# Where GpSimd's table scatters and early gathers stand among the powers of the layer norm

## The chip, the cores and the metric

The kernel runs on one core of one Trainium2 chip. A core has five engines with a queue of instructions each: TensorE (PE, with its weight loads, PEld), VectorE (DVE), ScalarE (ACT), GpSimd (POOL) and SyncE (SP). Each takes its own instructions strictly in order, and an instruction that waits for a semaphore holds up everything behind it on its engine. The metric is device time in microseconds (us) for one execution; lower is better.

## The reference: what is computed

Three layers run in a row on 4 x 576 = 2304 tokens of width 512.

```python
# 1. attention, 4 x 8 heads, 576 x 64; half of the heads look at the last 32 positions,
#    the other half at every 32nd
attn = softmax(where(mask, q @ k.T / 8, -1e9)); x = attn @ v      # -> (2304, 512)
# 2. dense layer of width 1024 with a soft gate and a layer norm
h = x @ w_in
solu = h * softmax(h)
ln = (solu - mean(solu)) / sqrt(var(solu) + 1e-6) * g_ln
x = ln @ w_out
# 3. eight experts, one per token
logits = x @ w_gate + modality_bias[modality_id]
e_idx = argmax(logits); gate_w = softmax(logits)[e_idx]
out[t] = gate_w[t] * (relu(x[t] @ w1[e_idx[t]]) @ w2[e_idx[t]])
```

## The kernel before, in words

The tokens are cut into 18 tiles of 128. The loop over `t` near the end of the function drives everything up to the experts: attention is spread over it in small slots, and iteration `t` does the first half of tile `t` and the second half of tile `t - 1`.

*First half* (`moe_a`, L463 to L497). PE computes `ph`, the product with `w_in`, in two halves of 12 matmuls. DVE takes the maximum (`hmx`) and its negative (`hnb`), ACT the exponential `e`, DVE the product `so` with its row sum.

*Second half.* `moe_stats` (L499 to L515) makes the layer norm's factors: ACT's square of `so` gives `var`, DVE makes `rstd`, **GpSimd raises it to the power -0.5 (L510)**, and DVE makes `sc` (L512) and `nm` (L514) from it. `moe_b_front` flips `so` on PE (`pn`), and ACT and DVE split it into `nH` and `nL`. `moe_b` (L529) multiplies by `w_out` on PE, into two PSUM tiles `pa` and `pb` of a pool with two buffers for both; ACT scales them by `sc` into `yt` (L541, L542), and DVE reads the gate's columns out of `pa` as `LG` (L543). The next tile's `pa` can't be written before that `LG` has been read. `yt` goes to `y_d` in DRAM.

*Routing.* After tiles 5, 11, 15 and 17 a group of 6, 6, 4 or 2 tiles is routed. `route_a` finds each token's expert, `route_b` (L592) its row in a table, and GpSimd writes one table row per token with an indirect transfer, one *scatter* per tile (L610). All scatters write `tab_d`, so each waits until the one before it has landed. After tile 11 the kernel chooses the expert that has most tokens so far. SP loads the first part of its list of tokens (`idxE`, L746) from the table, and GpSimd fetches their rows of `y_d` with four *gathers* into `xgE` (L824), which PE flips (`px`) in the last iteration, so that the first expert can start on them.

The order on each engine is set by the scheduler of the tile framework: it orders instructions by their dependences and a simulated timeline. `queue_after` (L715) adds a dependence without a semaphore: on the same engine, the later one is to be issued behind the earlier one. In the program before, nothing of that kind stands on scatters, gathers or powers.

Of the kernel before, what the change touches and what calls it, by code (L numbers as in the profile page):

```python
# [23 lines left out]
def indirect(ap):  # L24
    return bass.IndirectOffsetOnAxis(ap=ap, axis=0)
# [3 lines left out]
def tile_attention_moe_moe2(  # L29
# [19 lines left out]
    P = 128  # L49
# [413 lines left out]
    def moe_a(t, front, between):  # L463
# [32 lines left out]
                so[:, hf], e[:, hf], 1.0, hs[hf], ALU.mult, ALU.mult, accum_out=a2[:, hf:hf + 1])  # L496
        return so, e, s2, a2  # L497

    def moe_stats(so, e, s2, a2):  # L499
        nmu = st.tile([P, 1], F32, name="nmu")  # L500
        nc.vector.tensor_scalar(nmu, a2[:, 0:1], a2[:, 1:2], -1.0 / FF, ALU.add, ALU.mult)
        var = st.tile([P, 1], F32, name="var")
        nc.scalar.activation(e, so, AF.Square, bias=nmu, scale=1.0, accum_out=var)
        rs = st.tile([P, 1], F32, name="rs")
        nc.vector.tensor_scalar(rs, s2[:, 0:1], s2[:, 1:2], 1e-9, ALU.add, ALU.add)
        nc.vector.reciprocal(rs, rs)
        rstd = st.tile([P, 1], F32, name="rstd")
        nc.vector.tensor_scalar(rstd, rs, rs, 1.0 / FF, ALU.mult, ALU.mult)
        nc.vector.tensor_scalar(rstd, rstd, var, 1e-6, ALU.mult, ALU.add)
        nc.gpsimd.tensor_tensor(rstd, rstd, mhalf, ALU.pow)  # L510
        sc = st.tile([P, 1], F32, name="sc")
        nc.vector.tensor_tensor(sc, rstd, rs, ALU.mult)  # L512
        nm = st.tile([P, 1], F32, name="nm")
        nc.vector.tensor_tensor(nm, sc, nmu, ALU.mult)  # L514
        return sc, nm  # L515
# [76 lines left out]
    def route_b(t0, t1, tmp, eb):  # L592
        n = t1 - t0
        s = slice(t0, t1)
        pr = ps.tile([P, 6, NE], F32, name="pr", tag="T")
        nc.tensor.matmul(pr[:, :n], upper, OH[:, s], start=True, stop=False)
        nc.tensor.matmul(pr[:, :n], ones, CUM[:, s], start=False, stop=True)
        nc.vector.tensor_tensor(tmp[:, :n], pr[:, :n], OH[:, s], ALU.mult)
        rk = st.tile([P, 6], F32, name="rk")
        nc.vector.reduce_sum(rk[:, :n], tmp[:, :n], axis=AX.X)  # L600
        lo = st.tile([P, 6], I32, name="rlo")
        nc.vector.tensor_copy(lo[:, :n], rk[:, :n])
        hi = st.tile([P, 6], I32, name="rhi")
        nc.vector.tensor_scalar(hi[:, :n], lo[:, :n], 7, None, ALU.logical_shift_right)
        nc.vector.tensor_scalar(lo[:, :n], lo[:, :n], P - 1, None, ALU.bitwise_and)
        nc.vector.tensor_tensor(hi[:, :n], hi[:, :n], eb[:, :n], ALU.add)
        pos = st.tile([P, 6], I32, name="rpos")
        nc.vector.scalar_tensor_tensor(pos[:, :n], lo[:, :n], NTC, hi[:, :n], ALU.mult, ALU.add)
        for t in range(t0, t1):
            nc.gpsimd.indirect_dma_start(  # L610
                out=tab_d[:, :], out_offset=indirect(pos[:, t - t0:t - t0 + 1]),
                in_=entry[:, t], in_offset=None)

    mpstack = ExitStack()
    mp = mpstack.enter_context(tc.tile_pool(name="mp", bufs=2, side="right"))
# [204 lines left out]
        return w[3][f] if isinstance(w[3], list) else w[3][:, f]  # L820

    def gather(x, idx, j, rows=NT + 1, blocks=(0, 1)):
        for b in blocks:
            nc.gpsimd.indirect_dma_start(  # L824
                out=x[:, b], out_offset=None, in_=y_d[0:rows, :],
                in_offset=indirect(idx[:, 2 * j + b, 0:1].bitcast(U32)))

    def transpose_x(x, blocks=(0, 1), shift=0):
        for b in blocks:
            p = ps.tile([P, KD, P], F32, name="px", tag="T")  # L830
            for c in range(KD):
                flip_tile(p[:, c], x[:, b, c * P:(c + 1) * P], ident)
            s = slice((b + shift) * P, (b + shift + 1) * P)
            cp = nc.scalar.copy(gH[:, :, s], p)
            dv = nc.vector.tensor_tensor(gL[:, :, s], p, gH[:, :, s].bitcast(F32), ALU.subtract)  # L835
        return cp, dv
# [175 lines left out]
    for t in range(NTILE + 1):  # L1012
        bt = min((P * t + P - 1) // S, B - 1)
        take(4 * (16 * (bt + 1) + LAG))
        if taken >= QMAX and not done_att:
            done_att = True
            next(slots, None)
            atstack.close()
            wfst = ctx.enter_context(tc.tile_pool(name="wfst", bufs=1))
            W[0] = (wfst.tile([P, KD, FF], F32R, name="w1H"), wfst.tile([P, KD, FF], F32R, name="w1L"),  # L1020
                    wfst.tile([P, KF, DM], F32R, name="w2H"),
                    [x[:, i, 0:DM] for x in (xTH, xTL) for i in range(4)])

        def slot_bg(n=0):
            between()
            for _ in range(n):
                if background and W[0]:
                    background.pop(0)()

        if t == NTILE - 1:  # L1030
            while background:
                background.pop(0)()
            for j in range(EARLY):
                xgE[j] = rawp.tile([P, 2, DM], F32, name=f"xgE{j}", tag="raw")
                gather(xgE[j], idxE, j, 1 + EARLY_T * P)
        nT = []

        def front():
            if state and not nT:
                nT.extend(moe_b_front(state[1][0]))  # L1040

        cur = None
        if state:
            stats = moe_stats(*state[1])
        if t < NTILE:
            cur = (t, moe_a(t, front, slot_bg))
            reading[0] = t + 1
        front()
        slot_bg(1)
        if t == NTILE - 1:  # L1050
            transpose_x(xgE[0])
        if state:
            d = state[0]
            while wout or unfused:
                if unfused:
                    fuse_gate(*unfused.pop(0))
                if wout:
                    unfused.append(prep_w_out(wout.pop(0)))
            if d == 0:
                column_sums()  # L1060
            moe_b(d, *nT, *stats, slot_bg)
            if routed:
                route_b(*routed.pop())
            if d in (5, 11):
                routed.append((d - 5, d + 1, *route_a(d - 5, d + 1)))
            elif d == 15:
                routed.append((12, 16, *route_a(12, 16)))
            if d == EARLY_T - 1:
                choose_first()
                e_first = load_reg(infoE[0:1, 1:2], NE - 1, engines=[SP])  # L1070
                background = weight_steps(0, e_first)
                background.pop(0)()
            if d == EARLY_T + 2:
                load_idx(idxE, e_first)
        slot_bg(1)
        state = cur
    rt = route_a(16, 18)
    yo = mp.tile([P, 2, DM], F32, name="yoE", tag="e")
    chunk256(W[0], idxE, 0, ahead=lambda: route_b(16, 18, *rt), then=lambda: transpose_x(xgE[1]))
    choose_rest()  # L1080
    mpstack.close()
    e_r = [e_first] + [load_reg(info[0:1, NE + i:NE + i + 1], NE - 1, engines=[SP]) for i in range(1, NE)]
# [186 lines left out]
```

## Time and profile before

| | |
|---|---|
| median of 3 runs | 666.09 us (664.16 to 667.23) |
| profiled execution | 665.19 us, of which the span of the profile is 663.5 us |
| PE busy | 613.0 us, 92% of the span |
| PE weight loads busy | 551.2 us, 83% |
| DVE busy | 368.0 us, 55% |
| ACT busy | 320.7 us, 48% |
| POOL busy | 169.9 us, 26% |
| mean granted clock of PE | 0.972 |

The span is the time from the first to the last instruction. Since PE is busy for most of it, an instruction on another engine counts only where PE waits for it. The wait tables say how long an engine stood idle and whose semaphore came last; a timeline gives the same for one instruction, in brackets. PEclk is the share of TensorE's full clock that was granted in a stretch. An engine's row without a bracket started with no idle time before it.

### The profile page before, as it was taken

The page shows a single profiled execution, that of the slowest core. Times are in us where ns is not written, and L with a number is a line of the kernel's source. Part 1 is how long each engine was busy: PE and PEld are TensorE (multiplying, and loading weights), DVE is VectorE, ACT ScalarE, POOL GpSimd, SP SyncE. Part 2 cuts the span into 40 slices and gives each one's busy share as a digit, 9 for nine tenths or more (in the row PEclk, how much of TensorE's full clock was granted, in tenths as well). Part 3 has the DMA queues.
Part 4 walks back from the last instruction along what each step waited for, and adds up shares of the span by engine and source line. Part 5 has one row for each costly group of instructions (what it writes and reads, how often), then busy time and mean ns, then how long its engine had stood idle before and what let it go on. Part 6 is the DMA issues. An engine that isn't in the chain of part 4 may idle for free. (4 is left out here: it accounts for less than half of the span.)

```text
span 663.5 us, 12578 instructions
## 1 busy us (share of the span) xinstructions
PE 613.0 (92%) x4536; PEld 551.2 (83%) x4536; DVE 368.0 (55%) x1152; ACT 320.7 (48%) x709; POOL 169.9 (26%) x224
## 2 busy tenths in 40 slices
PE   6777989999999999999999699999899998999992
PEld 5666878999899987988889599889788887899892
DVE  5898788577767857677388353224454642221120
ACT  4898666566655657666275232223425352221220
POOL 2426455012432342111023203210120304012011
PEclk9997979999999999999999799999999999999997
DMA  8758221034111212110044200253636462012010
GB/s 221 178 152 219 75 82 37 21 85 117 52 53 40 78 49 57 53 35 16 17 159 128 80 33 18 68 178 123 198 112 223 126 211 88 27 55 64 17 49 24
DMA packets 54771, 59.98 MB, mean 90 GB/s; under 512 B 39312, under 2 KB 39312, under 8 KB 54674
## 3 DMA queue, kind: packets, MB, share of 16 engines
q1 hardware_dynamic: 47810, 42.52, 22.9%
q0 software_dynamic: 4272, 11.57, 5.5%
q10 hardware_dynamic: 2592, 4.72, 1.9%
q8 instruction: 47, 0.77, 0.5%
q14 instruction: 50, 0.41, 0.2%
HBM read 49.05 MB, written 10.26 MB: 89 GB/s over the span
## 5 line engine op out<-in xcount | busy, mean ns | idle before, releaser
L856 PE MATMUL py<-w2H,winL 128*128 128x512 f32 x288 | 92.0, 395 | 0.0
L896 PE MATMUL pf<-xTH,w1H 128*128 128x256 f32 x288 | 82.2, 286 | 3.1 <-DVE yo L995 2.1
L896 PE MATMUL pf<-xTL,w1H 128*128 128x256 f32 x288 | 81.6, 283 | 0.3 <-DVE xTL L835 0.3
L896 PE MATMUL pf<-xTH,w1L 128*128 128x256 f32 x288 | 81.4, 283 | 0.0
L903 DVE SCALAR_TENSOR_TENSOR winL<-pf,winL 128x512 fp32r<-128x512 f32 x36 | 24.9, 692 | 96.2 <-ACT winL L902 96.1
L368 POOL TENSOR_TENSOR ex<-ex,rd 96x384 f32<-96x384 f32 (+1 forms) x56 | 47.7, 852 | 108.3 <-DVE rd L362 64.0
L327 PE MATMUL S<-kz,qT 128*72 128x72 f32 (+1 forms) x448 | 59.2, 281 | 8.6 <-ACT kz L311 6.7
L902 ACT ACTIVATE winL<-pf 128x512 fp32r<-128x512 f32 x36 | 21.6, 599 | 87.9 <-PE pf L896 86.2
L856 PEld LDWEIGHTS py<-w2H,winL 128*128 128x128 f32 x288 | 53.4, 188 | 10.5
L327 PEld LDWEIGHTS S<-kz,qT 128*72 128x72 f32 (+1 forms) x448 | 51.1, 179 | 12.3 <-ACT kz L311 8.4
L480 PE MATMUL ph<-winH,xTH 128*128 128x512 f32 x144 | 59.5, 413 | 1.1 <-ACT xTH L400 0.8
L896 PEld LDWEIGHTS pf<-xTH,w1H 128*128 128x128 f32 x288 | 56.1, 195 | 4.6 <-issue 2.6
L480 PE MATMUL ph<-winL,xTH 128*128 128x512 f32 x144 | 57.9, 402 | 0.0
L896 PEld LDWEIGHTS pf<-xTL,w1H 128*128 128x128 f32 x288 | 56.2, 195 | 0.8 <-DVE xTL L835 0.5
L480 PE MATMUL ph<-winH,xTL 128*128 128x512 f32 x144 | 56.8, 401 | 0.0
L896 PEld LDWEIGHTS pf<-xTH,w1L 128*128 128x128 f32 x288 | 56.2, 195 | 0.0
L862 POOL DMA_INDIRECT out_dram<-yo,idx x14 | 14.1, 1006 | 146.6 <-ACT yo L861 122.8
L536 PE MATMUL pa<-woH,nH 128*128 128x264 f32 x144 | 43.1, 299 | 7.5 <-DVE LG L543 6.3
L536 PE MATMUL pa<-woH,nL 128*128 128x264 f32 x144 | 43.5, 302 | 0.2 <-DVE nL L526 0.2
L346 POOL TENSOR_TENSOR ex<-ex,mx 96x384 f32<-96x384 f32 (+1 forms) x32 | 24.9, 779 | 69.6 <-DVE mx L342 41.1
L357 DVE TENSOR_REDUCE den<-ex 72x4 f32<-72x292 f32 (+1 forms) x64 | 31.7, 497 | 19.2 <-ACT ex L349 10.2
L536 PE MATMUL pa<-woL,nH 128*128 128x264 f32 x144 | 41.9, 291 | 0.0
(244 smaller groups left out, 1601.7 us busy)
## 6 DMA issues: line engine op xcount, KB each, us to landing
raw<-in_moe_w_dram SPq DMA_DIRECT2D x36, 512.0 KB, 4.1
y_d<-yt ACTq DMA_DIRECT2D x18, 256.0 KB, 2.1
raw<-in_moe_w_in_dram SPq DMA_DIRECT2D x8, 512.0 KB, 6.9
raw<-in_moe_w_out_dram SPq DMA_DIRECT2D x8, 512.0 KB
vn<-in_v_dram SPq DMA_DIRECT2D x16, 160.0 KB, 3.8
qn<-in_q_dram SPq DMA_DIRECT2D x8, 288.0 KB
kn<-in_k_dram SPq DMA_DIRECT2D x8, 288.0 KB
vn<-in_v_dram SPq DMA_DIRECT2D x8, 288.0 KB
```

The source lines that it names most:

```text
L327: nc.tensor.matmul(sp_[:nq, i, :nk], qT[:, q0:q0 + nq], kT[:, half, k0:k0 + nk], start=True, stop=True)
L346: eng.tensor_tensor(ex[:nq, :nt, :nk], ex[:nq, :nt, :nk], mx[:nq, :nt].unsqueeze(2).to_broadcast([nq, nt, nk]), ALU.subtract)
L357: nc.vector.reduce_sum(den[:nq, :nt], exw[:nq, :nt, EPS:EPS + 1 + nk], axis=AX.X)
L368: nc.gpsimd.tensor_tensor(ex[:nq, :nt, :nk], ex[:nq, :nt, :nk], rd[:nq, :nt].unsqueeze(2).to_broadcast([nq, nt, nk]), ALU.mult)
L480: nc.tensor.matmul(ph, a[:, c, ts_], w[:, c, cs], start=n == 0, stop=n == 3 * KD - 1)
L536: nc.tensor.matmul(p, a[:, f], w[:, f, cols], start=n == 0, stop=n == 3 * KF - 1)
L856: nc.tensor.matmul(p, a[:, f, s], x, start=n == 0, stop=n == 3 * KF - 1)
L862: nc.gpsimd.indirect_dma_start(out=out[:, :], out_offset=indirect(idx[:, col, 2:3].bitcast(U32)), in_=o, in_offset=None, bounds_check=NT - ...
L896: mm = nc.tensor.matmul(p[:, u], a[:, c, fs], x[:, c], start=n == 0, stop=n == 3 * KD - 1)
L902: last[0] = (nc.scalar.activation(hH[:, f2s], p, AF.Relu), nc.vector.scalar_tensor_tensor(hL[:, f2s], p, 0.0, hH[:, f2s].bitcast(F32), ALU ...
L903: nc.vector.scalar_tensor_tensor(hL[:, f2s], p, 0.0, hH[:, f2s].bitcast(F32), ALU.max, ALU.subtract))
```

## The change

Two things are given an issue order on GpSimd. First, `route_b` no longer issues its scatters itself; it returns them as a list, and the loop puts them on `owed`. In each iteration, right after `moe_stats`, up to three of them (four in the last) are issued, and each is tied behind the power of that iteration (`pow_`). The last group, tiles 16 and 17, is issued as before. Second, the four gathers of `xgE` move from ahead of `moe_stats` in iteration 17 to behind it, and each is tied behind that iteration's power, which is the power of tile 16.

```diff
--- before.py
+++ after.py
@@ -496,6 +496,9 @@
                 so[:, hf], e[:, hf], 1.0, hs[hf], ALU.mult, ALU.mult, accum_out=a2[:, hf:hf + 1])
         return so, e, s2, a2
 
+    pow_ = [None]
+    owed = []
+
     def moe_stats(so, e, s2, a2):
         nmu = st.tile([P, 1], F32, name="nmu")
         nc.vector.tensor_scalar(nmu, a2[:, 0:1], a2[:, 1:2], -1.0 / FF, ALU.add, ALU.mult)
@@ -507,7 +510,7 @@
         rstd = st.tile([P, 1], F32, name="rstd")
         nc.vector.tensor_scalar(rstd, rs, rs, 1.0 / FF, ALU.mult, ALU.mult)
         nc.vector.tensor_scalar(rstd, rstd, var, 1e-6, ALU.mult, ALU.add)
-        nc.gpsimd.tensor_tensor(rstd, rstd, mhalf, ALU.pow)
+        pow_[0] = nc.gpsimd.tensor_tensor(rstd, rstd, mhalf, ALU.pow)
         sc = st.tile([P, 1], F32, name="sc")
         nc.vector.tensor_tensor(sc, rstd, rs, ALU.mult)
         nm = st.tile([P, 1], F32, name="nm")
@@ -606,10 +609,17 @@
         nc.vector.tensor_tensor(hi[:, :n], hi[:, :n], eb[:, :n], ALU.add)
         pos = st.tile([P, 6], I32, name="rpos")
         nc.vector.scalar_tensor_tensor(pos[:, :n], lo[:, :n], NTC, hi[:, :n], ALU.mult, ALU.add)
-        for t in range(t0, t1):
-            nc.gpsimd.indirect_dma_start(
+        def scatter(t):
+            return nc.gpsimd.indirect_dma_start(
                 out=tab_d[:, :], out_offset=indirect(pos[:, t - t0:t - t0 + 1]),
                 in_=entry[:, t], in_offset=None)
+
+        return [lambda t=t: scatter(t) for t in range(t0, t1)]
+
+    def scatters(n):
+        for _ in range(n):
+            if owed:
+                queue_after(owed.pop(0)(), pow_[0])
 
     mpstack = ExitStack()
     mp = mpstack.enter_context(tc.tile_pool(name="mp", bufs=2, side="right"))
@@ -820,10 +830,11 @@
         return w[3][f] if isinstance(w[3], list) else w[3][:, f]
 
     def gather(x, idx, j, rows=NT + 1, blocks=(0, 1)):
-        for b in blocks:
+        return [
             nc.gpsimd.indirect_dma_start(
                 out=x[:, b], out_offset=None, in_=y_d[0:rows, :],
                 in_offset=indirect(idx[:, 2 * j + b, 0:1].bitcast(U32)))
+            for b in blocks]
 
     def transpose_x(x, blocks=(0, 1), shift=0):
         for b in blocks:
@@ -1030,9 +1041,6 @@
         if t == NTILE - 1:
             while background:
                 background.pop(0)()
-            for j in range(EARLY):
-                xgE[j] = rawp.tile([P, 2, DM], F32, name=f"xgE{j}", tag="raw")
-                gather(xgE[j], idxE, j, 1 + EARLY_T * P)
         nT = []
 
         def front():
@@ -1042,6 +1050,12 @@
         cur = None
         if state:
             stats = moe_stats(*state[1])
+            scatters(4 if t == NTILE else 3)
+        if t == NTILE - 1:
+            for j in range(EARLY):
+                xgE[j] = rawp.tile([P, 2, DM], F32, name=f"xgE{j}", tag="raw")
+                for x in gather(xgE[j], idxE, j, 1 + EARLY_T * P):
+                    queue_after(x, pow_[0])
         if t < NTILE:
             cur = (t, moe_a(t, front, slot_bg))
             reading[0] = t + 1
@@ -1060,7 +1074,7 @@
                 column_sums()
             moe_b(d, *nT, *stats, slot_bg)
             if routed:
-                route_b(*routed.pop())
+                owed.extend(route_b(*routed.pop()))
             if d in (5, 11):
                 routed.append((d - 5, d + 1, *route_a(d - 5, d + 1)))
             elif d == 15:
@@ -1076,7 +1090,7 @@
         state = cur
     rt = route_a(16, 18)
     yo = mp.tile([P, 2, DM], F32, name="yoE", tag="e")
-    chunk256(W[0], idxE, 0, ahead=lambda: route_b(16, 18, *rt), then=lambda: transpose_x(xgE[1]))
+    chunk256(W[0], idxE, 0, ahead=lambda: [x() for x in route_b(16, 18, *rt)], then=lambda: transpose_x(xgE[1]))
     choose_rest()
     mpstack.close()
     e_r = [e_first] + [load_reg(info[0:1, NE + i:NE + i + 1], NE - 1, engines=[SP]) for i in range(1, NE)]
```

On GpSimd, at the first group of scatters (tiles 0 to 5), the order before is the following. `ex_...<-ex_...,rd` are divisions of attention, `rstd` is the power of a tile, here of tile 8.

```order
L368 TENSOR_TENSOR ex_125<-ex_125,rd 72x4x72
L610 DMA tab_d<-entry,rpos 22528x3 x5
L368 TENSOR_TENSOR ex_119<-ex_119,rd 96x3x128
L510 TENSOR_TENSOR rstd<-rstd,mhalf 128x1
L368 TENSOR_TENSOR ex_121<-ex_121,rd 96x3x128
L610 DMA tab_d<-entry,rpos 22528x3
L280 MEMSET vn 32x2x64
L368 TENSOR_TENSOR ex_123<-ex_123,rd 96x3x128
```

In the changed program the same place reads:

```order
L368 TENSOR_TENSOR ex_125<-ex_125,rd 72x4x72
L613 DMA tab_d<-entry,rpos 22528x3 x3
L368 TENSOR_TENSOR ex_119<-ex_119,rd 96x3x128
L513 TENSOR_TENSOR rstd<-rstd,mhalf 128x1
L613 DMA tab_d<-entry,rpos 22528x3
L368 TENSOR_TENSOR ex_121<-ex_121,rd 96x3x128
L613 DMA tab_d<-entry,rpos 22528x3 x2
L280 MEMSET vn 32x2x64
L368 TENSOR_TENSOR ex_123<-ex_123,rd 96x3x128
```

The power of tile 8 now stands behind three scatters instead of five, and the other three stand behind it.

On GpSimd, at the second group (tiles 6 to 11) and the early gathers, the order before is the following; the first two `rstd` rows are the powers of tiles 13 and 14, and the row of three those of tiles 15, 16 and 17.

```order
L510 TENSOR_TENSOR rstd<-rstd,mhalf 128x1
L610 DMA tab_d<-entry,rpos 22528x3
L510 TENSOR_TENSOR rstd<-rstd,mhalf 128x1
L610 DMA tab_d<-entry,rpos 22528x3 x5
L824 DMA xgE_5137<-y_d,idxE 128x512 x2
L824 DMA xgE_5140<-y_d,idxE 128x512 x2
L510 TENSOR_TENSOR rstd<-rstd,mhalf 128x1 x3
```

In the changed program:

```order
L513 TENSOR_TENSOR rstd<-rstd,mhalf 128x1
L613 DMA tab_d<-entry,rpos 22528x3
L513 TENSOR_TENSOR rstd<-rstd,mhalf 128x1
L613 DMA tab_d<-entry,rpos 22528x3 x5
L513 TENSOR_TENSOR rstd<-rstd,mhalf 128x1 x2
L834 DMA xgE_5152<-y_d,idxE 128x512 x2
L834 DMA xgE_5155<-y_d,idxE 128x512 x2
```

The second group stands as before, one scatter behind power 13 and five behind power 14. The four gathers have moved behind the powers of tiles 15 and 16, and only the power of tile 17 stands behind them.

On DVE the order before, from the second half of tile 16's `hmx` on; `sc` and the first `nm` are those of tile 15, `hnb` and `so` belong to tile 16.

```order
L484 TENSOR_REDUCE hmx<-ph 128x1
L526 TENSOR_TENSOR nL<-pn,nH 128x512
L489 TENSOR_SCALAR hnb<-hmx 128x1
L484 TENSOR_REDUCE hmx<-ph 128x1
L495 SCALAR_TENSOR_TENSOR so,a_5055<-e,ph 128x512
L512 TENSOR_TENSOR sc<-rstd,rs 128x1
L495 SCALAR_TENSOR_TENSOR so,a_5055<-e,ph 128x512
L505 TENSOR_SCALAR rs<-s_5052 128x1
L514 TENSOR_TENSOR nm<-sc,nmu 128x1
```

In the changed program:

```order
L484 TENSOR_REDUCE hmx<-ph 128x1
L529 TENSOR_TENSOR nL<-pn,nH 128x512
L515 TENSOR_TENSOR sc<-rstd,rs 128x1
L489 TENSOR_SCALAR hnb<-hmx 128x1
L517 TENSOR_TENSOR nm<-sc,nmu 128x1
L484 TENSOR_REDUCE hmx<-ph 128x1
L495 SCALAR_TENSOR_TENSOR so,a_5055<-e,ph 128x512 x2
```

`sc` of tile 15 has moved ahead of `hnb` and of the first `so` of tile 16, and `nm` ahead of both `so`. At the first group `sc` of tile 8 changes places with the reciprocal beside it. The orders of PE, ACT and SP are the same in both programs. Line numbers from L499 on are up to 14 higher in the changed program.

## Rows read from the trace of the kernel before

**Rows 1.** Waits of PE, 210 to 430 us: total us, times, longest.

```profile
PE pa L536 <- DVE LG L543: 6.3, 1, 6.3
PE S L327 <- ACT kz L311: 1.4, 1, 1.4
...
PE pa L536 <- DVE nL L526: 0.2, 1, 0.2
```

**Rows 2.** Three windows: length, busy time of each engine, granted clock (PEclk), DMA share.

```profile
371.00:377.00 6.00, 0.00 (x0) 0.00 (x0) 1.96 (x13) 2.62 (x6) 2.39 (x4) 0.69 0.40 126
381.00:383.00 2.00, 2.00 (x12) 2.00 (x11) 1.80 (x8) 0.53 (x2) 0.00 (x0) 0.50 0.00 0
545.00:565.00 20.00, 17.90 (x133) 16.06 (x132) 5.03 (x10) 6.29 (x14) 6.73 (x7) 1.00 0.37 113
```

**Rows 3.** Timeline of PE: start us, length us, what, idle before it and its releaser.

```profile
368.54 1.03 PE L129 MATMUL pn<-ident,so 128*128 128x128 f32 x8
...
377.23 0.56 PE L536 MATMUL pa<-woH,nH 128*128 128x264 f32 x1 [6.27 <-DVE LG L543]
...
383.41 0.32 PE L536 MATMUL pa<-woH,nL 128*128 128x264 f32 x1
...
388.39 0.66 PE L129 MATMUL px<-ident,xgE 128*128 128x128 f32 x4
```

**Rows 4.** Timeline of POOL, 343 to 390 us.

```profile
343.93 1.98 POOL L610 DMA_INDIRECT tab_d<-entry,rpos  x1 [3.88 <-DVE rstd L509]
...
362.98 0.96 POOL L610 DMA_INDIRECT tab_d<-entry,rpos  x1 [2.22 <-DMA tab_d<-entry,rpos]
367.81 0.98 POOL L824 DMA_INDIRECT xgE<-y_d,idxE  x1 [3.87 <-issue]
...
372.58 0.59 POOL L510 TENSOR_TENSOR rstd<-rstd,mhalf 128x1 f32<-128x1 f32 x1
376.01 0.55 POOL L510 TENSOR_TENSOR rstd<-rstd,mhalf 128x1 f32<-128x1 f32 x1 [2.84 <-DVE rstd L509]
386.51 0.59 POOL L510 TENSOR_TENSOR rstd<-rstd,mhalf 128x1 f32<-128x1 f32 x1 [9.95 <-DVE rdif L570]
```

**Rows 5.** Timeline of DVE, 343 to 390 us.

```profile
343.75 1.23 DVE L763 TENSOR_TENSOR w1L<-raw,w1H 128x1024 fp32r<-128x1024 f32 x1
...
360.96 0.20 DVE L509 TENSOR_SCALAR rstd<-rstd,var 128x1 f32<-128x1 f32 x1
...
362.27 0.20 DVE L489 TENSOR_SCALAR hnb<-hmx 128x1 f32<-128x1 f32 x1
...
363.32 0.69 DVE L495 SCALAR_TENSOR_TENSOR so<-e,ph 128x512 f32<-128x512 f32 x1 [0.25 <-ACT e L492]
...
373.20 0.16 DVE L512 TENSOR_TENSOR sc<-rstd,rs 128x1 f32<-128x1 f32 x1 [9.18 <-POOL rstd L510]
373.28 0.68 DVE L495 SCALAR_TENSOR_TENSOR so<-e,ph 128x512 f32<-128x512 f32 x1
...
376.86 0.22 DVE L543 SCALAR_TENSOR_TENSOR LG<-pa,sc,BI 128x8 f32<-128x8 f32 x1
...
386.15 0.21 DVE L509 TENSOR_SCALAR rstd<-rstd,var 128x1 f32<-128x1 f32 x1 [0.15 <-ACT e L503]
```

**Rows 6.** SP's issue of the index load; landing times of gathers, then of scatters.

```profile
365.09 0.33 SPq L746 DMA_DIRECT2D idxE<-tab_d  x1
...
DMA to landing us min/median/max: 3.7/3.7/3.7
...
DMA to landing us min/median/max: 2.1/2.5/5.4
```

**Rows 7.** Timeline of POOL and DVE around the first group of scatters.

```profile
246.48 0.58 POOL L510 TENSOR_TENSOR rstd<-rstd,mhalf 128x1 f32<-128x1 f32 x1
...
247.09 0.78 DVE L512 TENSOR_TENSOR sc<-rstd,rs 128x1 f32<-128x1 f32 x1 [4.16 <-POOL rstd L510]
...
251.54 0.82 POOL L368 TENSOR_TENSOR ex<-ex,rd 96x384 f32<-96x384 f32 x1 [1.64 <-DVE rd L362]
```


## The prediction

> **What bounds the kernel now.** The page first: PE is busy 92% of a span of 663.5 us, so time is won only where PE stands still or runs at less than its full clock. The slices of the granted clock show one fall in the middle of the run. The table of PE's waits in the stretch of the last tiles says who is behind it: one wait of 6.3 us, of `pa` on DVE's `LG`, and nothing else above 1.4 us [rows 1]. The windows give its second half: in the gap the clock averages 0.69, and two microseconds after PE's return it is still 0.50, that is 1.2 instead of 2.4 GHz [rows 2]. The timeline of PE gives the edges: the gap of 6.27 us ends at 377.23, so it began at 370.96, and the slow matmuls last to 383.41 [rows 3].
>
> Who held `LG`? DVE's rows lead there: `rstd` of tile 15 was ready for its power at 361.16 (360.96 + 0.20), and `sc`, which needs that power, started at 373.20 after an idle of 9.18 us that POOL's `rstd` ended [rows 5]. POOL's rows tell why: the last of the six scatters of tiles 6 to 11 starts at 362.98, then come four gathers from 367.81 on, and the power of tile 15 starts right behind them at 372.58 without any idle of its own [rows 4]. The first gather waited 3.87 us behind the last scatter. Its indices come from a transfer that SP issued at 365.09, when that scatter had landed [rows 6]. So POOL's queue stood on a DMA while a 0.6 us power, ready since 361.16, waited behind it; the other tiles' chain, DVE and at last PE waited for that.
>
> **The change, part by part.** By the instruction order three things move, and nothing moves on PE, ACT or SP.
>
> *The gathers behind power 16.* POOL now has scatter, power 15, power 16, four gathers, power 17. The order has power 15 directly behind the sixth scatter, which ends at 362.98 + 0.96 = 363.94 [rows 4]. That is later than 361.16, so the power starts at 363.94 instead of 372.58. From the start of the power to `sc` is 373.20 - 372.58 = 0.62 us, so `sc` comes at 364.56. On DVE `sc` also moves up one place, ahead of `hnb` of tile 16, and `hnb` must now wait for it: 364.6 instead of 362.27. From `hnb` to the first `so` was 1.05 us (362.27 to 363.32), so the first `so` is at 365.7; the second follows by 0.6, at 366.3, where it was at 373.28 [rows 5]. That second `so` heads what follows in one chain (its statistics, power 16, `sc`, `LG`, then PE), so all of this comes 7.0 us earlier. PE's release at 377.23 becomes 370.25. PE runs out of other work at 370.96: 0.7 us of slack, and the gap of 6.27 closes. The chain also needs PE's flips `pn`, done by 368.54 + 1.03 = 369.57 [rows 3], in time for a release at 370.25. PE's short wait on `nL` behind it, 0.2 us [rows 1], stays about as it is, since `nL` hangs on the same chain.
>
> *The clock.* Without the gap the fall of the clock goes too. The nearest row is a stretch with 2.1 us of PE idle (545 to 565) at a granted clock of 1.00, against 0.69 in the gap [rows 2]; what stays here is some tenths. From 377.23 to 383.41 PE did 6.18 - 0.23 = 5.95 us of work at half clock (the wait on `nL` taken off), so 2.98 us come back. Bounds: 0 if the clock falls anyway, 2.98 if it doesn't. I take 2.98, since the idle that stays is nearest to the row at 1.00.
>
> *What the moved gathers now hold up.* Power 16 moves from 376.01 to 369.0, so the first gather can start at about 369.6, 1.8 us later than at 367.81; its indices were there by then. Four gathers took 372.58 - 367.81 = 4.77 us, which puts their end at 374.4. Queued behind them is power 17. Its `rstd` starts at 386.15 [rows 5], with PE 9.25 us earlier at 376.9: 2.5 us of slack. The data: PE flips `xgE` at 388.39 [rows 3], then at 379.1. The second gather, issued at 370.9 and landing 3.7 us later [rows 6], is there at 374.6: 4.5 us of slack. The cover of both moves is thus PE's own work of a tile. SP's queue is not touched.
>
> *The first group of scatters (tiles 0 to 5).* Before, five scatters stood in POOL's queue ahead of power 8, which ran at 246.48; `sc` of that tile waited 4.16 us for it [rows 7]. Now three stand ahead, and three come behind it. The order puts each scatter behind the landing of the one before, so the power comes two scatters earlier, at most 4.16 us. PE did not wait for this: its only wait nearby is 1.4 us, of the scores on ACT's copy of `kz` [rows 1], on the attention chain that queues behind `sc` on DVE. Bounds: a gain of 1.4 if all of this wait was due to the late power; on the other side the next division that now stands behind the last three scatters. It starts at 251.54, and with landings at the median of 2.5 us the sixth scatter is over some 3 us before that; were two landings as long as the longest, 5.4 us [rows 6], it would be late by about 3 and PE with it. I take +0.5: a part of the 1.4, nearer to the median landing.
>
> *The rest.* Although the words of the change say three at a time, the order leaves the second group as it was (one scatter behind power 13, five behind power 14), and the third. These cost and give nothing.
>
> The sum: 6.27 + 2.98 + 0.5 = 9.75 us. The profiled execution took 665.19 us (a span of 663.5 and 1.7 around it), which gives 655.4; the median of the runs before is 666.09, 0.9 higher, and the same sum from there gives 656.3. I forecast the median.
>
> **A rule that speaks against it.** The scatter at 343.93 took 1.98 us, beside DVE's `w1L` of 128x1024 at 343.75; the scatter at 362.98, with DVE nearly idle, took 0.96 [rows 4, 5]. Before, the four gathers ran while DVE stood still; now they run while DVE works on tile 16. The Trainium skill, SBUF — State Buffer, section "Who interferes with whom", says that DVE and GpSimd share one pair of ports and that a DVE operation with two inputs in SBUF, or in a two-port mode, blocks GpSimd for its whole length; these two rows agree with it. By it the move has a price, which the second rival works out from the rows.
>
> **The rivals.**
> 1. *The gap closes and the clock falls all the same*, from the tenths that stay or the attention flips around it. For it: the clock fell within this gap. Against: 2.1 us of idle elsewhere at 1.00 [rows 2]. Then only 6.27 + 0.5 are won: 659.3.
> 2. *A new wait behind the gathers.* If each of the four takes 1.98 instead of 0.96 us, plus the 0.3 between them, they need 9.1 us and end at 378.7; power 17 is then 1.6 us late, and the `sc` of tile 17 holds `nL` in DVE's queue, for which PE waits. Gain 9.75 - 1.6: 657.9. Against: only some of DVE's work there is of that kind.
> 3. *The sixth scatter is late.* The five steps from 343.93 to 362.98 hang on landings. Each microsecond beyond the slack of 0.7 reopens the gap, and from some 3 us the clock falls with it: a gain of about 3, or 663.
> 4. *Slower.* The same at its worst: `sc` of tile 15 now stands ahead of `hnb` of tile 16 in DVE's queue, so a late scatter holds up that tile's whole softmax. With every step at 5.7 us (the longest landing and 0.3) the sixth scatter starts at 372.4, power 15 at 373.4, and PE is released 6.3 us behind it, at 379.7: 2.5 us later than before, 668.5. It decides from a power 15 at 371, seven microseconds later than this trace has it. Only one landing in 18 was that long.
> 5. *The change doesn't do what it says*: already so for two of three groups. For the gathers the order shows that it does.
>
> **How the numbers follow.** Forecast 0.77; first rival 0.08; second 0.08; third 0.04; fourth, with anything else that costs, 0.03. About 0.5% (3.3 us) is what a measurement of this kernel can tell from no change. The forecast, the first two rivals end below 662.8: with a part of the third that is 0.93 for faster; 0.05 for within 0.5%; 0.02 for slower. The range: down to 666.09 - 9.25 - 1.4 - 1.5 (half the spread of the three runs, 664.16 to 667.23) = 653.9; up past the first two rivals to 660.0. Beyond it lie the third and the fourth, and the edges of the first.
>
> **What would show it.** Right: power 15 directly behind the sixth scatter at about 364, `sc` 0.6 us later, no wait of PE on `LG` above 1 us, a clock of 1.00 through tiles 15 to 17, gathers from about 369.6, power 17 and the flips of `xgE` without a wait. Wrong: power 15 far from the last scatter; a wait of PE on `nL` or on `xgE` that was not there; half-rate matmuls though the gap is gone. In the first group `sc` should come some 4 us earlier, and the wait on `kz` should shrink.

## The result, and the profile after

The changed kernel took 658.42 us (median of 4 runs, 656.32 to 659.16), against 666.36 us for the kernel before in the same session (4 runs, 664.16 to 667.23). The ratio is 0.9881, with an interval of 0.9848 to 0.9914. That is faster by 1.2%. The forecast was 656.3 us in a range of 653.9 to 660.0; the gain is 7.9 us where the sum had 9.75. By its time alone this result lies nearer to the first two rivals (659.3 and 657.9) than to the forecast; the traces below tell them apart. The profiled execution took 658.36 us with a span of 656.6 us.

Read first PE's waits from 210 to 430 us in the changed kernel (total us, times, longest). The wait of 6.3 us on `LG`, first line of [rows 1], is gone; what is new is small: 0.7 on `nL` where it was 0.2. The line of `kz` holds two waits: the one that was 1.42 us is 0.83, and one of 0.49 at 235 us, which stood in the trace before as well, under "issue".

```profile
PE S L327 <- ACT kz L311: 1.3, 2, 0.8
PE pa L539 <- ACT nH L528: 1.2, 3, 0.7
PE ph L480 <- ACT xTH L400: 0.8, 1, 0.8
PE pa L539 <- DVE nL L529: 0.7, 1, 0.7
```

POOL's timeline of the changed kernel (start, length, what, idle before and its releaser) shows why, beside [rows 4]. The power of tile 15 starts at 364.55 directly behind the sixth scatter, the power of tile 16 at 369.62, and the four gathers only then. Ahead of the power of tile 17 POOL stands idle for 2.55 us and waits for DVE, which made `rstd` at 377.62 (the bracket names `rdif`, right behind it), and not for the gathers.

```profile
363.56 0.96 POOL L613 DMA_INDIRECT tab_d<-entry,rpos  x1 [3.43 <-DMA tab_d<-entry,rpos]
364.55 0.57 POOL L513 TENSOR_TENSOR rstd<-rstd,mhalf 128x1 f32<-128x1 f32 x1
369.62 0.55 POOL L513 TENSOR_TENSOR rstd<-rstd,mhalf 128x1 f32<-128x1 f32 x1 [4.51 <-DVE rstd L512]
370.66 1.02 POOL L834 DMA_INDIRECT xgE<-y_d,idxE  x1 [0.49 <-ACT nH L528]
371.98 0.95 POOL L834 DMA_INDIRECT xgE<-y_d,idxE  x1 [0.30 <-issue]
...
374.49 0.95 POOL L834 DMA_INDIRECT xgE<-y_d,idxE  x1 [0.30 <-issue]
377.99 0.60 POOL L513 TENSOR_TENSOR rstd<-rstd,mhalf 128x1 f32<-128x1 f32 x1 [2.55 <-DVE rdif L573]
```

DVE's timeline of the changed kernel, to be read against [rows 5]: the idle time ahead of `sc` of tile 15 is 3.79 instead of 9.18 us, the second `so` starts at 366.95 instead of 373.28, and `LG` at 370.47 instead of 376.86.

```profile
359.96 0.20 DVE L512 TENSOR_SCALAR rstd<-rstd,var 128x1 f32<-128x1 f32 x1
...
365.14 0.16 DVE L515 TENSOR_TENSOR sc<-rstd,rs 128x1 f32<-128x1 f32 x1 [3.79 <-POOL rstd L513]
365.22 0.21 DVE L489 TENSOR_SCALAR hnb<-hmx 128x1 f32<-128x1 f32 x1
...
366.95 0.69 DVE L495 SCALAR_TENSOR_TENSOR so<-e,ph 128x512 f32<-128x512 f32 x1
...
370.20 0.16 DVE L515 TENSOR_TENSOR sc<-rstd,rs 128x1 f32<-128x1 f32 x1 [0.72 <-POOL rstd L513]
...
370.47 0.22 DVE L546 SCALAR_TENSOR_TENSOR LG<-pa,sc,BI 128x8 f32<-128x8 f32 x1
```

PE's timeline of the changed kernel at the place of [rows 3]: the products of `pa` are held up only for `nL`, by 0.70 us, and the flips of `xgE` run at 379.85 without a wait. (In the second and the third trace of this kernel they wait 0.30 us, for DVE's `nL` and not for a gather.)

```profile
372.31 0.39 PE L539 MATMUL pa<-woH,nL 128*128 128x264 f32 x1 [0.70 <-DVE nL L529]
...
379.85 0.66 PE L129 MATMUL px<-ident,xgE 128*128 128x128 f32 x4
```

Windows of the changed kernel (length, busy us of PE, PEld, DVE, ACT, POOL, granted clock, DMA share, GB/s). Around the old gap the clock is 1.00 throughout, where [rows 2] had 0.69 and 0.50. But 95 us later, in the experts, it falls to 0.52 for some 3.5 us. The last row is the matmul behind which that begins; its wait of 1.96 us is on a branch of ACT's sequencer.

```profile
366.00:372.00 6.00, 5.60 (x43) 5.11 (x41) 3.98 (x17) 3.85 (x10) 1.58 (x3) 1.00 0.02 2
372.00:378.00 6.00, 5.70 (x48) 5.70 (x49) 4.85 (x19) 3.19 (x8) 2.84 (x4) 1.00 0.77 219
...
464.00:466.00 2.00, 0.47 (x3) 0.47 (x4) 0.00 (x0) 0.35 (x1) 0.00 (x0) 1.00 0.77 172
466.00:468.00 2.00, 2.00 (x14) 2.00 (x13) 0.00 (x0) 0.19 (x1) 0.00 (x0) 0.62 0.60 236
468.00:470.00 2.00, 2.00 (x11) 2.00 (x11) 0.00 (x0) 0.20 (x1) 0.49 (x1) 0.52 0.01 2
470.00:472.00 2.00, 2.00 (x19) 2.00 (x18) 0.04 (x1) 0.83 (x3) 0.49 (x1) 1.00 0.35 135
```

```profile
465.53 0.39 PE L950 MATMUL pq<-winH,xTH 128*128 128x256 f32 x1 [1.96 <-ACTq L1246]
```

**Where the time went, by stage.** Spans of one and the same kernel differ (656.6, 654.5 and 652.6 in three traces of the changed one; in the start alone these three vary by 3.1 us below), so a pair of traces can't be subtracted as a whole. I cut each trace at marks that every kernel has on POOL: the first scatter of the first group, the power of tile 13, the first scatter of the third group, the first and the ninth scatter of results to `out_dram`, and the end. The lengths in us, worked out from the POOL timelines of all traces:

```
trace                    start  first group  gathers' stage  results  experts  end
before                  233.34       106.12           58.18    24.28    86.73  154.85
e4_before_again         232.88       106.05           57.11    24.28    88.82  154.26
e10_before_third        233.77       106.04           58.52    24.28    87.12  154.17
after                   234.30       105.31           49.48    24.28    88.68  154.55
e1_after_again          232.01       105.31           49.46    24.27    88.95  154.50
e9_after_third          231.22       105.30           48.91    24.28    88.94  153.95
e2_gathers_only         233.36       107.21           49.55    24.28    88.86  157.04
e3_scatters_only        235.21       105.26           57.34    24.28    88.58  156.23
e5_gathers_behind_15    235.40       105.25           53.41    24.28    88.42  154.94
e6_two_each             232.25       105.29           48.50    24.28    88.86  155.82
e8_two_each_again       233.96       105.31           48.80    24.28    88.75  154.00
```

From the mean of the three traces of before to the mean of the three of after: the gathers' stage gives 57.94 - 49.28 = 8.65 us, the first group 106.07 - 105.31 = 0.76, and the experts take back 88.86 - 87.56 = 1.30. That is 8.1, and the three timed comparisons of this kernel gave 7.9 to 8.5 (1.19% to 1.28% of 666; the bare medians differ by 7.9, 8.9 and 9.2). The start varies within one kernel (231.22 to 234.30) nearly as much as over all of them (231.22 to 235.40); the end is some 2 us longer in e2 and e3 than in most, since PE's clock fell once more there, behind waits of 2.00 and 2.15 us (more on such falls below).

### The profile page after: what moved, and what is told of

It reads as the page before. It is cut to its first block, busy times and chain, and to the rows that moved or that the text cites. A ratio compares the mean times of both kernels' runs of the same rounds, so it can differ in the third digit from the quotient of the medians.

```text
span 656.6 us, 12578 instructions
## 1 busy us (share of the span) xinstructions
PE 610.1 (93%) x4536; PEld 548.7 (84%) x4536; DVE 367.7 (56%) x1152; ACT 320.9 (49%) x709; POOL 169.8 (26%) x224
## 5 line engine op out<-in xcount | busy, mean ns | idle before, releaser
L539 PE MATMUL pb<-woH,nL 128*128 128x256 f32 x144 | 41.1, 285 | 0.0
```

The lines of the kernel that those rows point to most:

```text
L539: nc.tensor.matmul(p, a[:, f], w[:, f, cols], start=n == 0, stop=n == 3 * KF - 1)
```

## The experiments

Each ratio is to the kernel before in the same session; the second and third traces of before are single runs.

**1. The change again, and each half alone.** First the unchanged kernels a second time, to know what a repetition is worth, then the gathers' part without the scatters' part, and the other way round.

> The changed kernel once more. Place theory: the gain is made between 230 and 390 us, about 9.5 us there (first group 0.8, gathers 8.7), and what the time shows less than that is lost to falls of the granted clock in other places (the first 60 us, and near 466) that come and go from run to run; so this trace should again have no PE wait on LG and a clock of 1.00 through tiles 15 to 17, but may have other falls elsewhere. Time 656 to 659. Rival: the falls near 30 and 466 belong to the changed program; then both are here again, at the same places, 1.7 us near 466.

Measured: 657.05 us (655.44 to 660.45), ratio 0.9876 (0.9839 to 0.9912). No wait on `LG`, as the theory says; but both falls were there again at the same places, half clock from about 16 to 40 us and near 466, as the rival says. The further traces part the two. Half clock from 16 to 40 us also shows in the second trace of before and not in the third of the changed kernel, so it does not belong to the change. The fall near 466 stays open (below).

> The kernel before once more, for its trace alone. Theory: the gap of about 6.3 us at 371 and the half clock behind it are there again; the falls of the clock in the first 100 us stand at other places than in the first trace. If the fall behind a 2 us wait is a matter of the moment and not of the program, one may show here too, for example near 474.

Measured: 665.12 us, span 663.4; the wait of PE on `LG` was 5.3 us and the gathers' stage 57.11, one microsecond less than in the first trace. The sixth scatter's time varies by so much (22.60 us behind power 13, instead of 23.52). And the clock did fall behind a wait of 2.02 us at 472.56, where it had stayed at 1.00 in the first trace.

Gathers alone, against the changed kernel (scatters issued at once, as before):

```diff
-                owed.extend(route_b(*routed.pop()))
+                for x in route_b(*routed.pop()):
+                    x()
```

> Only the four gathers are moved behind power 16; all scatters are issued as before the change. Theory: the gathers carry nearly all; 657 to 660, no PE wait on LG, and the 4.2 us wait of sc for power 8 is there as before. Rival (the scatters carry the gain): 665 to 666.

Measured: 658.34 us (657.69 to 662.02), ratio 0.989 (0.9856 to 0.9924). The gathers' stage is 49.55 us, as with the whole change, and POOL's timeline of this kernel has the same rows: power, power, and the gathers behind them. The wait of `sc` for power 8 is there, 5.29 us where 4.2 were expected.

```profile
364.23 0.96 POOL L613 DMA_INDIRECT tab_d<-entry,rpos  x1 [2.11 <-DMA tab_d<-entry,rpos]
365.21 0.57 POOL L513 TENSOR_TENSOR rstd<-rstd,mhalf 128x1 f32<-128x1 f32 x1
370.28 0.55 POOL L513 TENSOR_TENSOR rstd<-rstd,mhalf 128x1 f32<-128x1 f32 x1 [4.50 <-DVE rstd L512]
371.32 1.02 POOL L834 DMA_INDIRECT xgE<-y_d,idxE  x1 [0.49 <-ACT nH L528]
```

Scatters alone, against the changed kernel (gathers back ahead of `moe_stats`, with no order on them):

```diff
+            for j in range(EARLY):
+                xgE[j] = rawp.tile([P, 2, DM], F32, name=f"xgE{j}", tag="raw")
+                gather(xgE[j], idxE, j, 1 + EARLY_T * P)
...
-        if t == NTILE - 1:
-            for j in range(EARLY):
-                xgE[j] = rawp.tile([P, 2, DM], F32, name=f"xgE{j}", tag="raw")
-                for x in gather(xgE[j], idxE, j, 1 + EARLY_T * P):
-                    queue_after(x, pow_[0])
```

> Only the scatters are tied behind powers; the gathers stay ahead of power 15. Theory: 665.0 to 666.0, a gain of 0.4 to 1.4, with the PE wait of 6.3 us on LG and the half clock behind it as before. Rival (the scatters carry the gain): below 660.

Measured: 665.57 us (663.67 to 668.61), ratio 0.9988 (0.9963 to 1.0014). Of PE's waits between 210 and 430 us, the one on `LG` is back, while the one on `kz` is 0.8 as with the whole change:

```profile
PE pa L539 <- DVE LG L546: 6.4, 1, 6.4
...
PE S L327 <- ACT kz L311: 0.8, 1, 0.8
```

So the gathers' part carries the gain. The scatters' part gives the 0.8 us of the first group (105.26 against 106.07), and that is too little for the timing to tell from nothing. Where the gathers were changed alone, this stage is even 1.1 us longer than before (107.21): there the third scatter started 3.47 us behind the second instead of 2.40, with power 8 still behind five of them. That this late landing cost the 1.1 us is read from one trace and was not tested.

**2. Does it matter behind which power the gathers stand?** Their loop moves ahead of `moe_stats` in the same iteration, where `pow_` still holds the power of tile 15: the same tie, but power 16 then queues behind them.

```diff
+            for j in range(EARLY):
+                xgE[j] = rawp.tile([P, 2, DM], F32, name=f"xgE{j}", tag="raw")
+                for x in gather(xgE[j], idxE, j, 1 + EARLY_T * P):
+                    queue_after(x, pow_[0])
...
-        if t == NTILE - 1:
-            for j in range(EARLY):
...
```

> As the changed kernel, but the four gathers stand between powers 15 and 16 instead of behind both: a smaller dose of the old wait. Power 16, ready some 30 us behind power 13, must wait for the gathers' end about 3 us later, and LG behind it. Theory: PE waits 2.3 to 3.0 us on LG there; the stretch from power 13 to the third group's first scatter is longer than the changed kernel's 49.5 us by this wait and, where the clock falls behind it, by up to 3 us more: 52 to 55. Time 660 to 663. Rival (power 15 alone held the chain, power 16 does not matter): no wait on LG, 49.5 us, 657 to 658.5.

Measured: 661.43 us (657.17 to 663.44), ratio 0.9924 (0.9895 to 0.9953); the gathers' stage is 53.41 us, 3.9 longer than in the change's first trace. POOL's timeline, then PE's, then two windows of this kernel: power 16 waits behind the fourth gather until 373.07; PE waits 2.15 us for `LG` (2.3 to 3.0 expected); and from about 1.6 us behind that the clock is at 0.50, and 0.67 in the second window (from 380 on it is 1.00).

```profile
364.46 0.57 POOL L513 TENSOR_TENSOR rstd<-rstd,mhalf 128x1 f32<-128x1 f32 x1
368.24 1.02 POOL L834 DMA_INDIRECT xgE<-y_d,idxE  x1 [3.21 <-issue]
...
372.09 0.96 POOL L834 DMA_INDIRECT xgE<-y_d,idxE  x1 [0.30 <-issue]
373.07 0.57 POOL L513 TENSOR_TENSOR rstd<-rstd,mhalf 128x1 f32<-128x1 f32 x1
```

```profile
374.32 0.36 PE L539 MATMUL pa<-woH,nH 128*128 128x264 f32 x1 [2.15 <-DVE LG L546]
```

```profile
376.00:378.00 2.00, 2.00 (x10) 2.00 (x10) 1.12 (x4) 0.82 (x3) 0.00 (x0) 0.50 0.33 124
378.00:380.00 2.00, 2.00 (x13) 2.00 (x13) 1.89 (x8) 0.62 (x2) 0.00 (x0) 0.67 0.00 0
```

The 3.9 us are accounted for: 2.15 of wait, and 2 x 0.50 + 2 x 0.33 = 1.7 of clock. The chain as the prediction read it (power, `sc`, `so`, next power, `sc`, `LG`, PE) is what sets PE's release: it was lengthened at its second power, and PE waited.

**3. The clock by itself.** In the kernel *before*, the chain is left as late as it was, and PE is given work in the gap: 30 more products (`FILL`) into the PSUM tile of tile 15's second half of flips. Other than expected below, what they add is not zero: they change the result from tile 15 on, and may change its routing; so only the time up to the third group's scatters is read here, not the experts' stretch or the whole time.

```diff
+            if fronts[0] == 15 and g == 1:
+                for i in range(FILL):
+                    nc.tensor.matmul(
+                        pt.rearrange("p a b -> p (a b)"), winH[:, i % KD, 0:P],
+                        zeros.bitcast(F32R).to_broadcast([P, 512]), start=False, stop=i == FILL - 1,
+                        skip_group_check=True)
```

> The kernel before, with 30 matmuls on a column of zeros added to the flips of tile 15 (they add zero and cost 6.8 us of PE at full clock), so that PE works where it stood still; powers, scatters and gathers stand as before the change. The scheduler moves the six matmuls that PE did ahead of the gap (1.4 us) behind it. Theory (the clock falls because PE stands still): the wait on LG shrinks to about 1 us, the chain on POOL and DVE stays as late as before, the clock is 1.00 through 369 to 385, and about 3.0 - 1.4 = 1.6 us are won: 664 to 665. Rival (the clock falls there for another reason): half-rate matmuls behind 377 as before, and 667 to 668.

Measured: 666.72 us (663.28 to 668.96), ratio 1.0011 (0.9983 to 1.0039). That is not the 664 to 665 expected and close to the rival's 667; but since the kernel computes something else from tile 15 on, its whole time decides nothing. POOL's timeline, then PE's, then two windows: the power of tile 15 is as late as before, 372.60; the added products fill 6.80 us, PE's wait on `LG` shrinks to 1.05, and the clock stays at 1.00 where it had been at 0.50.

```profile
372.60 0.59 POOL L511 TENSOR_TENSOR rstd<-rstd,mhalf 128x1 f32<-128x1 f32 x1
```

```profile
369.39 6.80 PE L529 MATMUL pn<-zeros,winH 128*128 128x512 f32 x30
...
377.25 0.37 PE L546 MATMUL pa<-woH,nH 128*128 128x264 f32 x1 [1.05 <-DVE LG L553]
```

```profile
369.00:377.00 8.00, 7.20 (x36) 6.01 (x34) 1.93 (x12) 2.44 (x5) 3.98 (x5) 1.00 0.48 131
...
380.00:383.00 3.00, 3.00 (x28) 3.00 (x27) 0.00 (x0) 0.47 (x1) 0.00 (x0) 1.00 0.02 5
```

The gathers' stage was 56.60 us, 1.3 less than the mean of before, with the products' work in it and with a wait on `nL` of 0.95 instead of 0.23. So in this trace, with the chain as late as before and no gap, the clock did not fall: its fall was the gap's doing, and it came on top of the gap.

**4. Without the dependence on the sixth scatter.** Two scatters behind each power instead of three, and the first expert's list loaded one iteration step later, so that the second group reads one behind power 13, three behind 14 and two behind 15.

```diff
-            scatters(4 if t == NTILE else 3)
+            scatters(4 if t == NTILE else 2)
...
-            if d == EARLY_T + 2:
+            if d == EARLY_T + 3:
```

> As the changed kernel, but two scatters instead of three are issued behind each power, so that the last two of the second group stand behind power 15, and the load of the indices is issued one iteration later. Theory: power 15 then starts when its rstd is ready, about 22 us behind power 13 instead of 24.5 to 25; hnb of tile 16 is no longer held up and the wait of PE on nL goes from 0.7 to 0.2 or less: the stretch from power 13 to the third group is 48.8 to 49.3 us instead of 49.5, time 656.5 to 658, not to be told from the changed kernel. Rival: the later indices make the gathers late and PE waits for xgE: 50 us or more.

Measured: 654.8 us (654.24 to 658.74), ratio 0.984 (0.98 to 0.9879). POOL's timeline of this kernel: power 15 now waits for DVE's `rstd`, not for a landing, and so does power 16; the gathers start at 366.93. The wait on `nL` is gone, as expected; the stage, 48.50 us, and the time came out lower than expected.

```profile
358.97 0.57 POOL L513 TENSOR_TENSOR rstd<-rstd,mhalf 128x1 f32<-128x1 f32 x1 [2.74 <-DVE rstd L512]
359.74 1.03 POOL L613 DMA_INDIRECT tab_d<-entry,rpos  x1 [0.19 <-issue]
362.19 0.96 POOL L613 DMA_INDIRECT tab_d<-entry,rpos  x1 [1.42 <-DMA tab_d<-entry,rpos]
364.41 0.57 POOL L513 TENSOR_TENSOR rstd<-rstd,mhalf 128x1 f32<-128x1 f32 x1 [1.26 <-DVE rstd L512]
366.93 1.02 POOL L834 DMA_INDIRECT xgE<-y_d,idxE  x1 [1.95 <-issue]
```

It and the changed kernel were then run side by side on one chip, with the kernel before beside them:

> Two scatters behind each power, once more, beside the changed kernel on the same chip. Theory: the stretch from power 13 to the third group's first scatter is 48.5 us again (49.5 in the changed kernel), so about 1 us is won on it: 654.5 to 657, ratio to the kernel before 0.982 to 0.988. Rival: the lower median of the first time was the spread of the runs; then no difference to the changed kernel on this chip.

> The changed kernel for a third time, beside two scatters behind each power. Theory: 49.5 us from power 13 to the third group, no wait on LG, 656 to 659; the experts' stretch from the first scatter of results to the ninth takes 88.5 to 89 us when the clock falls behind the 2 us wait near 466, and about 86.7 when it does not.

> The kernel before for a third trace: a wait on LG of 5 to 6.5 us, 57 to 58.2 us from power 13 to the third group. The experts' stretch takes 86.7 or 88.5 to 89 us, as the clock behind its 1.8 to 2.0 us wait falls or not.

Measured: two each 656.07 us (653.41 to 657.56), ratio 0.9852 (0.9815 to 0.9888); the changed kernel 656.38 us (654.28 to 659.84), ratio 0.9872 (0.9832 to 0.9912); before 665.62 us, with a wait on `LG` of 6.55 and a gathers' stage of 58.52 us, a little above what was expected. The gathers' stage is 48.50 and 48.80 us with two each, against 48.91 to 49.48 with the change. So the dependence on the sixth scatter costs some 0.6 us of that stage in the mean (49.28 - 48.65; the later load of the list is in it too); the version with two each is the best of those run by its medians, but the intervals overlap and the timing does not tell the two apart.

## Why the prediction was right, and where its sum was off

**The chain: right.** Power 15 directly behind the sixth scatter (364.55, forecast 363.94), `sc` 0.59 later, the second `so` at 366.95 (366.3), `LG` read by 370.69 (release forecast 370.25), no wait of PE on `LG`. Everything came some 0.5 us later than forecast, for two reasons: the whole trace ran 0.15 later (power 13 at 339.61 instead of 339.46), and the landings took 0.43 more (the sixth scatter 23.95 us behind power 13, instead of 23.52). The slack of 0.7 covered it for `LG`. The prediction left open whose `LG` it was: by DVE's order it is tile 14's, whose `sc` had been made at 347.48, and which only stands in DVE's queue behind the `sc` of tile 16. To move it ahead there was not tried.

**The gap and the clock in it: right, 8.65 in the mean instead of 9.25.** Between the first traces of the two kernels the stage gave 8.70. In this pair the term that was off is the wait on `nL`, put at 0.2 and measured at 0.70: this is 0.5 of the 0.55 that are missing. It goes with the late landings above, since `nL` hangs on the chain that has no slack: it was 0.70, 0.32 and nothing where the sixth scatter came 23.95, 23.54 and 22.93 us behind power 13 (after, e1, e9). In e9 the stage gave 9.27 against the first trace of before. But e1 won no more than the first trace: there, as in e9, PE waited some 0.5 instead of 0.28 us for ACT's `nH` of the next tile, and 0.30 at the flips of `xgE`, which the prediction had without a wait. In the mean over three traces of each kernel PE's wait on `LG` went from 6.0 us to nothing (6.27, 5.30 and 6.55 before) and its other waits in this stage from 0.5 to 1.0; of the 8.65 us this leaves 8.65 - 6.0 + 0.5 = 3.1 for the clock, an estimate. The clock's term of 2.98 thus held, and the filled gap showed its cause.

**The clock elsewhere: not foreseen, -1.3.** The argument of that term was weaker than its number. The row of 545 to 565 us in [rows 2] holds one single wait of PE, 2.10 us on DVE's `yo`, and the clock stayed at 1.00 behind it. That is true, but it is one case, and I read it as a rule. The eleven traces (without that of the filled gap) hold 22 single waits of PE of 1.5 to 2.4 us behind 240 us; here they are by length, with the clock two to three us after the wait's end, from PE's timelines and windows behind each:

```
wait us  1.50 1.53 1.55 1.58 1.63 1.76 1.82 1.85 1.86 1.87 1.96 1.98 2.00 2.02 2.04 2.07 2.09 2.10 2.15 2.15 2.15 2.37
clock    1.00 1.00 1.00 1.00 1.00 1.00 0.50 0.50 1.00 1.00 0.50 0.50 0.50 0.50 0.50 0.50 0.50 1.00 0.50 0.50 0.50 1.00
```

Twelve of the 22 were followed by half clock, and between 1.8 and 2.4 us the length alone doesn't decide: 2.10 and 2.37 stayed at full clock, 1.82 did not. Two of the rows, from PE's timelines of before and of the gathers alone, both waits on `yo`, with products of the same kind (`py` and `px` ahead, `pf` behind) on both sides; the first is the one that the prediction rested on, the second was followed by 0.50:

```profile
557.79 0.37 PE L896 MATMUL pf<-xTH,w1H 128*128 128x256 f32 x1 [2.10 <-DVE yo L995]
```

```profile
517.78 0.36 PE L907 MATMUL pf<-xTH,w1H 128*128 128x256 f32 x1 [2.00 <-DVE yo L1006]
```

Eleven of the waits are the one on ACT's branch ahead of `pq` in the experts, one in each trace. Of the three traces of before, two stayed at full clock there (1.76 and 1.87) and one fell (2.02); all three of the changed kernel fell (1.96, 2.15 and 2.09), and so did the five of the other variants (1.82 to 2.07). The experts' stretch has 86.73 and 87.12 us where the clock stayed and 88.42 to 88.95 where it fell: a fall costs some 1.8 us, and the first pair of traces lost 1.95 of the gain in this place, 95 us behind the change. Whether the changed kernel always falls there, because its wait is some tenths longer, or whether before merely escaped it twice, three traces of each can't settle. The first rival (the gap closes and the clock falls all the same) had this only around the gap, and there it did not happen; a fall in another stage stands in no term and no rival of the prediction.

**The first group: right in sign, 0.76 instead of 0.5.** `sc` of tile 8 came at 243.65 instead of 247.09; measured from the first scatter of the group that is 9.35 instead of 13.75 us, 4.4 earlier (forecast: some 4). PE's wait on `kz` went from 1.42 to 0.83. The other bound, a late division, did not happen, though POOL had no time to spare: the sixth scatter ran at 250.44 behind a landing that had kept POOL idle for 3.16 us, and the division started right behind it, at 251.57, which is 17.27 us behind the group's first scatter instead of 18.20.

```profile
243.05 0.57 POOL L513 TENSOR_TENSOR rstd<-rstd,mhalf 128x1 f32<-128x1 f32 x1
...
250.44 0.96 POOL L613 DMA_INDIRECT tab_d<-entry,rpos  x1 [3.16 <-DMA tab_d<-entry,rpos]
251.40 0.22 POOL L280 MEMSET vn<- 32x128 f32 x1
251.57 0.84 POOL L368 TENSOR_TENSOR ex<-ex,rd 96x384 f32<-96x384 f32 x1
```

**The second rival, gathers slowed by DVE: did not happen.** The four took 1.02, 0.95, 0.95 and 0.95 us while DVE was busy for 4.02 of 4.90 us (370.60 to 375.50), and power 17 kept its slack (2.55 us idle; forecast 2.5). DVE's work beside the last three gathers was `nL`, `hmx` and `so`, which read PSUM. Only the first ran beside operations with two inputs in SBUF, the two `yt` here, and it took 1.02 us where the first gather of before, with DVE idle, had taken 0.98.

```profile
370.61 0.51 DVE L549 SCALAR_TENSOR_TENSOR yt<-csum,nm,yt 128x256 f32<-128x256 f32 x1
371.18 0.47 DVE L549 SCALAR_TENSOR_TENSOR yt<-csum,nm,yt 128x256 f32<-128x256 f32 x1
```

The Trainium skill (SBUF — State Buffer, "Who interferes with whom") says of such an operation that it contends with a GpSimd instruction that reads SBUF; the prediction took this as a block for its whole length, and for this gather the measurement does not show that. The step that failed in this rival is that all four gathers would pay what the scatter beside `w1L` paid [rows 4, 5]. The scatters on record show what that price hung on. In ten of the twelve traces `w1L` had started 0.17 or 0.18 us ahead of the second group's first scatter, which then took 1.98 or 1.99 us. In the two others `w1L` started behind it, by 0.10 (e4) and 0.03 us (e5, the rows below), and it took 1.06. So the price went with which of the two had started first, and not with the kind of operation alone.

```profile
345.05 1.06 POOL L613 DMA_INDIRECT tab_d<-entry,rpos  x1 [3.82 <-DVE rstd L512]
345.08 1.23 DVE L773 TENSOR_TENSOR w1L<-raw,w1H 128x1024 fp32r<-128x1024 f32 x1 [0.19 <-ACT w1H L772]
```

**The third and fourth rivals, a late sixth scatter:** the third is present at its smallest, as the 0.5 us on `nL`; the version with two scatters behind each power took it away. Its "from some 3 us the clock falls" no run shows: behind the wait of 2.15 us on `LG` at this very place (experiment 2) the clock fell already. In none of the traces did the landings come near what the fourth needs. **The fifth:** two of the three groups of scatters were indeed left as they were. The gathers' gain did not need them, but something was lost by it: with the second group spread as well (two behind each power) its stage was some 0.6 us shorter in the two runs of experiment 4.

**The sum:** 8.65 + 0.76 - 1.30 = 8.1 us measured by stages against 6.27 + 2.98 + 0.5 = 9.75 forecast. The mechanism and the largest terms held; a half microsecond of short waits (`nL`, `nH`, the flips of `xgE`), and a clock that falls in another stage, are the difference (the first group gave 0.3 more than its term). The time still fell inside the range because that was drawn up past the first two rivals, and not because the prediction knew of the 1.30 us in the experts.

## What to carry to other kernels

On an engine that issues in order, a short operation that a long chain hangs on should not queue behind one that waits for a transfer: the four gathers cost PE some 9 us where they stood and 4 us one power too early, while behind the power of tile 16 no wait of PE led back to them. The order of issue is worth tying exactly there, and a change that only spreads such waits where PE hardly waits for them (the scatters) is worth tenths. When a gap is priced, add the matmuls at half clock that follow it, and read the clock behind every other single wait of a microsecond or two as well, stage by stage over several traces, before a gain of 1% is subtracted from two spans.

## What the runs showed of the hardware

That PE waits as short as 1.82 us are followed by matmuls at 1.2 instead of 2.4 GHz, in 12 of 22 cases between 1.5 and 2.4 us, I had expected only of gaps like that of 6.27 us; behind the wait of 1.96 us in the changed kernel PE ran at or near half rate until 470. What sets apart the cases of like length (2.09 and 2.10) no run here shows. The chained scatters of one row per token start 2.4 us apart at the best (237.59, 239.99, 242.35 and 244.72 in the kernel before), and the longest single step in a row took 6.0 (349.14 to 355.17 in e8), which is why a short operation behind several of them in one queue comes at a time that varies from trace to trace.
